# Four of a unit's sixteen gram copies on ScalarE are moved behind the copies of the second layer's sums

## The chip, the cores and the metric

The kernel runs as one program on one core of a Trainium2 chip. The metric is the device time of one execution in microseconds (us); lower is better. The engines are TensorE (PE in the profile, with PEld for its weight loads), VectorE (DVE), ScalarE (ACT), GpSimd (POOL) and SyncE (SP, which issues most transfers).

## What is computed

The reference chains three layers over 3072 tokens. Attention with a delta-rule state runs over 4 batches, 8 heads, 768 steps and 48 columns per head; a gated dense layer (384 to 1536 to 384) follows; a routed layer with eight experts and a skip test ends it. Cut to what matters:

```python
for t in range(S):                       # per batch and head, state [48, 48]
    y[t] = q[t] @ state
    v_old = state @ kn[t]                # kn: k, made unit length
    state = state + beta[t] * outer(kn[t], v[t] - v_old)

gate = sigmoid(x @ w_gate)               # x: y of all heads, [3072, 384]
x = (gate * (x @ w_val)) @ w_out

kept = x @ w_skip > 0                    # tokens that go through an expert
e = argmax(x @ w_gate2)                  # one of eight
out = x;  out[kept] += p_e * (relu(x @ w1[e]) @ w2[e])
```

All inputs and outputs are float32.

## The kernel before

The tokens are cut into 12 units of 256 tokens: 64 steps of each of the 4 batches. A loop over units `u` (in `program`, from 1 to 11) does, in each turn, twelve steps `f` of the dense layer of unit `u`, with the attention of later units and the routing of earlier ones woven in.

The dense layer, in each step: `first` (L863) multiplies the unit's x by the step's part of both up-weights into a PSUM tile gv (two buffers). `gate` takes it out: ACT makes sg, the sigmoid (L873), DVE multiplies it by the other half (L874), ACT rounds it to gh (L876), POOL makes the rest gl (L877). `second` (L886, L889) multiplies gh and gl by the out-weights and adds into two PSUM tiles acc, [128, 394] each, which are summed over all twelve steps. `second` runs two steps behind (`LAG = 2`). So the last two steps of unit `u - 1` come in steps 0 and 1 of unit `u`, and the first `second` of unit `u`, which overwrites acc, comes in step 2.

The routing of unit `u - 1` starts in step 1, behind that last `second` (in the first turn in step 0): ACT copies both acc tiles to x1 (L902, called x in the profile), POOL stores x1 to out (L896, two DMAs of 192 KB) and to xa (L923), and DVE works on it (L914 to L922 and, in step 3, L929 to L937).

The attention of unit `u + 2` starts in step 0 with `grams`: PE makes four PSUM tiles gram_0 to gram_3, all in one row of 64 matmuls (L300). ACT takes them out in the order 0, 2, 1, 3 with four copies each: two into g (L306), which SP then sends to DRAM as scr_g (L316), and two over the queries kq (L310), which POOL multiplies by a mask (L311). `blocks` brings scr_g back as bt (L331), and `solve` inverts small triangular blocks in it on DVE, in pieces that `spend` gives out over the steps; its last piece writes xx (L393). In step 0 of the next turn, the rest of an unfinished solve is run first. SP sends xx as scr_t (L397) and places it back as tt (L401, four DMAs). `combine`, in steps 2 to 4 of that turn, needs tt: DVE transposes it to dn (L588), PE multiplies to m1p (L594) and later to x2p (L604).

The masked kq are not read before `chain` of that unit, a turn later.

What sets the order: the loop is written under `in_order` for PE, DVE and ACT, so each of the three runs its instructions as a scheduler laid them out, from priority bands and a timeline, and waits for each in turn. SP and POOL have one queue each too. A wait holds all that stands behind it on that engine.

Of the kernel before, what the change touches and what calls it, by code (L numbers as in the profile page):

```python
# [17 lines left out]
AF = mybir.ActivationFunctionType  # L18
ALU = mybir.AluOpType
# [156 lines left out]
def sl(a, n):  # L176
    return slice(a, a + n)


class Attention:  # L180
# [90 lines left out]
    def keep(self, u, c, ps):  # L271

        nc = self.k.nc
        i, cc = divmod(c, 2)
        qp = self.u[u]["qp"][i]
        mask = self.k.c("mask").rearrange("p (a t) -> p a t", a=1).to_broadcast([128, 4, 64])
        for p, h in ((slice(64, 128), 0), (slice(0, 64), 1)):
            q = qp[p, cc, :, h, :]
            if u < KEEPA:
                nc.scalar.activation(q, ps[p, :, h, :], AF.Copy)  # L280
                nc.gpsimd.tensor_tensor(q, q, mask[p], op=ALU.mult)
            else:
                nc.vector.tensor_tensor(q, ps[p, :, h, :], mask[p], op=ALU.mult)

    def grams(self, u, tags):


        k, nc, p = self.k, self.k.nc, self.p
        d = self.u[u]
        g = d["g"] = p.tile([128, CPU_, 4, 64], F32, name=f"g{u}", tag="g", bufs=1)  # L290
        mask = k.c("mask").rearrange("p (a t) -> p a t", a=1).to_broadcast([128, 4, 64])
        for cc in range(2):
            ps = [k.ps_a.tile([128, 4, 2, 64], F32, name=f"gram{u}_{2 * i + cc}", tag=tags[2 * cc + i], bufs=1)
                  for i in range(2)]
            for pr in range(4):
                for i in range(2):
                    kt, kq = d["kt"][i], d["kq"][i]
                    for par in range(2):
                        r0, o0 = 64 * par, 64 * (1 - par if i == 0 else par)
                        nc.tensor.matmul(  # L300
                            ps[i][o0:o0 + 64, pr], kt[r0:r0 + 48, cc, pr, :], kq[r0:r0 + 48, cc, pr, par:par + 2],
                            start=True, stop=True)
            for i in range(2):
                for par in range(2):
                    r, o = sl(64 - 64 * par, 64), sl(64 * (1 - par if i == 0 else par), 64)
                    nc.scalar.activation(g[r, 2 * i + cc], ps[i][o, :, 1 - par, :], AF.Copy)  # L306
                for par in range(2):
                    r, o = sl(64 - 64 * par, 64), sl(64 * (1 - par if i == 0 else par), 64)
                    q = d["qp"][i][r, cc, :, par, :]
                    nc.scalar.activation(q, ps[i][o, :, par, :], AF.Copy)  # L310
                    nc.gpsimd.tensor_tensor(q, q, mask[r], op=ALU.mult)  # L311
        sg = self.scr_g[u % 2]
        for par in range(2):
            for blk in range(2):
                o0 = 64 * (1 - par) + 32 * blk
                nc.sync.dma_start(  # L316
                    sg[par, blk].rearrange("n m t -> m n t"),
                    g[o0:o0 + 32].rearrange("p c h t -> p (c h) t")[:, :, sl(32 * blk, 32)])

    def blocks(self, u, place=None, other=None):  # L320

        k, nc, p = self.k, self.k.nc, self.p
        d = self.u[u]
        if place is None:
            d["bt"] = p.tile([128, 32, 32], F32, name=f"bt{u}", tag="bt", bufs=1)
        else:
            d["bt"] = place
        first = None
        d["be"] = p.tile([128, 32], F32, name=f"be{u}", tag="be", bufs=2)
        for h2 in range(2):  # L330
            dma = (nc.sync, other or nc.sync)[h2].dma_start(  # L331
                d["bt"][sl(64 * h2, 64)], self.scr_g[u % 2].rearrange("r b n m t -> (r b n) m t"))
            first = first or dma
        for h2 in range(2):
            (other or nc.sync).dma_start(d["be"][sl(64 * h2, 64)], k.io["beta"][:, u])
        return first.ins
# [943 lines left out]
def drain(g):  # L1280
    for _ in g:
        pass
# [12 lines left out]
def program(ctx, tc, io, out):  # L1295
    k = Kernel(ctx, tc, io, out)
    k.setup()
    m1 = Moe1(k)
    xp = k.pool("xt")
    at = Attention(k)  # L1300
    dctx = ExitStack()
    m1.dp = k.pool("decode", ctx=dctx)
    nc = k.nc
# [221 lines left out]
    def between():  # L1525
# [10 lines left out]
        if GO == 0:  # L1536
            yield from grams(range(CPU_))
        early = third()
        for cs in ((0, 1), (2, 3)):
            if GO == 1:  # L1540
                yield from grams(cs)
            with k.band("prep"):
                for c in cs:
                    at.spread(1, c)
                gens = [at.double(1, c, k.ps_a, tags[(DT // 10, DT % 10)[c % 2]], 1) for c in cs]
            for _ in range(4):
                with k.band("prep"):
                    for g in gens:
                        next(g)
                yield  # L1550
            with k.band("prep"):
                turns(*gens)
            if GO == 2:
                yield from grams(cs)
# [51 lines left out]
    def spend(pieces, time):  # L1606

        pieces[1] += time
        with k.band("solve"):
            while pieces[1] > 0:  # L1610
                pieces[1] -= pieces[2]
                pieces[2] = next(pieces[0], 99)

    def load(u):
        with k.band("prep"):
            for i in range(2):
                at.load(u, i, (2 * u + i) % 4)

    def second():
        with k.band("second"):  # L1620
            m1.second(*behind.popleft())
# [3 lines left out]
    with k.in_order(*engines[0:3]):  # L1625
        for u in range(1, NU):
            more = u + 1 < NU
            if more:
                with k.band("top"):
                    xs[u + 1] = xp.tile([128, 2, KT3, UT], F32R, name=f"x{u + 1}", tag="x", bufs=2)  # L1630
                chain = at.chain(u + 1, xs[u + 1], "prep")
            join = at.combine(u + 1) if 2 < u + 1 < NU else iter(())
            route = m1.route(u - 1)
            for f in range(NF):
                with k.band("main"):
                    fp = m1.first(u, f, xs[u])
                with k.band("gate"):
                    g = m1.gate(*fp)
                    q = next(g)
                    drain(g)  # L1640
                if f == RANKF:
                    with k.band("route"):
                        drain(route)
                if f == GRAMF:
                    spend(solve, 99)
                if f == GRAMF and u + 2 < NU:
                    with k.band("prep"):
                        at.grams(u + 2, ("prep", "y", "rw", "s"))
                        at.blocks(u + 2)
                    solve = [at.solve(u + 2), 0, 1.1]  # L1650
                if f == JOINF - 1:
                    with k.band("prep"):
                        next(join, None)
                if f < JOINF or f > JOINF + 1:
                    spend(solve, SPEND[f])
                if more:
                    if f == JOINF:
                        with k.band("prep"):
                            next(join, None)
                        with k.band("top"):  # L1660
                            next(chain)
                    if f == JOINF + 1:
                        with k.band("prep"):
                            drain(join)
                if f in (JOINF, JOINF + 1):
                    spend(solve, SPEND[f])
                if more:
                    if f in WHEN:
                        with k.band("top"):
                            for _ in range(WHEN[f]):  # L1670
                                next(chain, None)
                    if f == LOADF and u + 3 < NU:
                        load(u + 3)
                    if f == LOADF and 2 < u + 2 < NU:
                        with k.band("prep"):
                            at.beside(u + 2)
                behind.append(q)
                if len(behind) > LAG:
                    second()
                if f == (LAG - 1 if u > 1 else 0):  # L1680
                    with k.band("route"):
                        next(route)
                        next(route)
            if u + 2 == NU:
                at.ctx.close()
                m2 = Moe2(k, m1)
        while behind:
            second()
# [114 lines left out]
```

## Time and profile before

| | |
|---|---|
| time, median of 3 runs | 933.21 us (931.25 to 935.35) |
| the profiled execution | 939.17 us, span 937.4 us |
| PE busy in the span | 843.2 us (90%) |
| DVE | 646.3 us (69%) |
| ACT | 424.4 us (45%) |
| POOL | 344.7 us (37%) |
| granted TensorE clock, mean | 0.962 |

The profiled execution is slower than the median of the unprofiled runs by some 6 us. The span is counted from its first instruction; the nine units that have grams start at about 206, 258, 310, 361, 411, 462, 514, 564 and 616, and the text calls a unit by that. In a timeline, a row is a time of start, a length, an engine, a line of the listing, what is written and read, and how many instructions were merged; the bracket at the end is the idle time of that engine before it and what ended that. A row without a bracket followed the one before it on its engine with no idle time worth naming. The share of busy time says little here: ACT is busy 45% of the time, and the rows are about one place where others stand behind it.

### The profile page before, as it was taken

The page shows a single profiled execution, that of the slowest core. Times are in us where ns is not written, and L with a number is a line of the kernel's source. Part 1 is how long each engine was busy: PE and PEld are TensorE (multiplying, and loading weights), DVE is VectorE, ACT ScalarE, POOL GpSimd, SP SyncE. Part 2 cuts the span into 40 slices and gives each one's busy share as a digit, 9 for nine tenths or more (in the row PEclk, how much of TensorE's full clock was granted, in tenths as well). Part 3 has the DMA queues.
Part 4 walks back from the last instruction along what each step waited for, and adds up shares of the span by engine and source line. Part 5 has one row for each costly group of instructions (what it writes and reads, how often), then busy time and mean ns, then how long its engine had stood idle before and what let it go on. Part 6 is the DMA issues. An engine that isn't in the chain of part 4 may idle for free.

```text
span 937.4 us, 26573 instructions
## 1 busy us (share of the span) xinstructions
PE 843.2 (90%) x10833; PEld 804.7 (86%) x10833; DVE 646.3 (69%) x1869; ACT 424.4 (45%) x998; POOL 344.7 (37%) x411
## 2 busy tenths in 40 slices
PE   6249797899889999999999999999899989999996
PEld 5247686789889999999989998999899988999996
DVE  6837785837959686878879796869622237877674
ACT  6365366354253535354443535353233235555452
POOL 6202564325261625344342616252322432412511
PEclk9999779779999999999999999999989999999999
DMA  8492303203343433333343434340200196766610
GB/s 191 138 366 84 80 2 111 51 3 76 77 107 81 103 81 64 86 68 86 83 103 78 109 78 104 84 101 15 61 3 15 48 340 202 252 206 218 213 55 15
DMA packets 132428, 99.29 MB, mean 106 GB/s; under 512 B 88231, under 2 KB 111868, under 8 KB 132304
## 3 DMA queue, kind: packets, MB, share of 16 engines
q1 hardware_dynamic: 125264, 78.44, 30.8%
q0 software_dynamic: 6624, 18.81, 6.6%
q8 instruction: 86, 1.41, 0.7%
q14 instruction: 38, 0.31, 0.1%
q10 hardware_dynamic: 416, 0.33, 0.1%
HBM read 76.66 MB, written 18.61 MB: 102 GB/s over the span
## 4 chain that ended last, share of the span: by engine, by line
PE 58%; DVE 17%; DMA 8%; ACT 7%; issue 6%; POOL 2%; SPq 2%; ACTq 0%; POOLq 0%; DVEq 0%
PE gv L863 22%; PE acc L886 9%; PE poe L1069 6%; PE he L1052 6%; PE acc L889 4%; DMA raw<-in_w 2%; ACT g L306 2%; DMA tt<-scr_t 2%; ACT kq L310 2%; PE y L714 2%; DVE tmp L386 2%; DVE sg L874 1%; DVE xx L391 1%; DVE dec L793 1%; PE x2p L604 1%
## 5 line engine op out<-in xcount | busy, mean ns | idle before, releaser
L863 PE MATMUL gv<-x,w 128*128 128x256 f32 x2592 | 349.1, 289 | 9.2 <-ACT w L802 3.6
L863 PEld LDWEIGHTS gv<-x,w 128*128 128x128 f32 x2592 | 339.6, 196 | 11.7 <-DVE sg L874 3.8
L877 POOL TENSOR_TENSOR gl<-sg,gh 128x256 fp32r<-128x256 f32 x144 | 114.2, 794 | 338.3 <-ACT gh L876 316.9
L886 PE MATMUL acc<-w,gh 128*128 128x394 f32 x576 | 138.7, 361 | 13.1 <-ACT x L902 8.1
L876 ACT ACTIVATE gh<-sg 128x256 fp32r<-128x256 f32 x144 | 60.2, 418 | 155.7 <-DVE sg L874 155.2
L874 DVE TENSOR_TENSOR sg<-sg,gv 128x256 f32<-128x256 f32 x144 | 60.0, 417 | 90.2 <-ACT sg L873 89.5
L873 ACT ACTIVATE sg<-gv 128x256 f32<-128x256 f32 x144 | 55.1, 383 | 139.3 <-PE gv L863 117.4
L886 PEld LDWEIGHTS acc<-w,gh 128*128 128x128 f32 x576 | 96.9, 192 | 20.5 <-ACT x L902 9.7
L386 DVE TENSOR_TENSOR tmp<-xx,bt 128x126 f32<-128x126 f32 (+28 forms) x299 | 95.7, 325 | 6.5
L391 DVE TENSOR_TENSOR xx<-xx,tmp 128x126 f32<-128x126 f32 (+28 forms) x299 | 87.3, 297 | 8.9
L889 PE MATMUL acc<-w,gl 128*128 128x394 f32 x288 | 77.8, 351 | 4.3 <-POOL gl L877 4.3
L971 DVE TENSOR_TENSOR w2le<-rawe,w2he 128x768 fp32r<-128x768 f32 x66 | 63.1, 955 | 10.6 <-ACT w2he L970 8.8
L311 POOL TENSOR_TENSOR kq<-kq,consts 64x256 f32<-64x256 f32 x72 | 55.5, 770 | 16.9 <-ACT kq L310 12.2
L889 PEld LDWEIGHTS acc<-w,gl 128*128 128x128 f32 x288 | 54.5, 194 | 5.0 <-POOL gl L877 4.9
L970 ACT ACTIVATE w2he<-rawe 128x768 fp32r<-128x768 f32 x66 | 55.4, 840 | 2.3 <-DMA rawe<-in_w 2.1
L803 POOL TENSOR_TENSOR w<-dec,w 128x576 fp32r<-128x576 f32 x24 | 31.5, 1330 | 62.2 <-ACT w L802 49.5
L1052 PE MATMUL he<-x2he,w2he 128*128 128x256 f32 x168 | 48.4, 288 | 1.9 <-DVE tgg L1159 1.4
L1060 ACT ACTIVATE hhe<-he 128x256 fp32r<-128x256 f32 x64 | 24.5, 383 | 50.6 <-PE he L1052 33.9
L1052 PE MATMUL he<-x2le,w2he 128*128 128x256 f32 x168 | 47.3, 282 | 0.0
L1052 PE MATMUL he<-x2he,w2le 128*128 128x256 f32 x168 | 47.1, 280 | 0.0
L1078 POOL DMA_INDIRECT out<-ote,tis x16 | 16.3, 1018 | 81.5 <-DVE ote L1077 77.1
L1069 PE MATMUL poe<-w2he,hhe 128*128 128x384 f32 x128 | 43.3, 338 | 0.0
(333 smaller groups left out, 1491.3 us busy)
## 6 DMA issues: line engine op xcount, KB each, us to landing
rawe<-in_w SPq DMA_DIRECT2D x64, 384.0 KB, 4.4
raw<-in_w SPq DMA_DIRECT2D x24, 576.0 KB, 6.2
kq<-in_kq SPq DMA_DIRECT2D x44, 192.0 KB, 5.1
kv<-in_kv SPq DMA_DIRECT2D x22, 384.0 KB, 5.9
xa<-x POOLq DMA_DIRECT2D x12, 392.0 KB
out<-x POOLq DMA_DIRECT2D x24, 192.0 KB
bt<-scr_g SPq DMA_DIRECT2D x18, 256.0 KB, 5.0
xx<-in_eye SPq DMA_DIRECT2D x9, 256.0 KB
```

The lines of the kernel that those rows point to most:

```text
L311: nc.gpsimd.tensor_tensor(q, q, mask[r], op=ALU.mult)
L386: v.tensor_tensor(t, x[:, :ni, m:m + 1].to_broadcast([128, ni, b - a]), bt[:, m:m + 1, m + 1 + a:m + 1 + b].to_broadcast([128, ni, b - a]) ...
L391: v.tensor_tensor(x[:, :ni, m + 1 + a:m + 1 + b], x[:, :ni, m + 1 + a:m + 1 + b], t, op=ALU.add)
L863: nc.tensor.matmul(gv[:, j], self.part(f, j, w)[:, c], y[:, a], start=n == 0, stop=n == 8)
L874: nc.vector.tensor_tensor(sg, sg, gv[:, 1], op=ALU.mult)
L876: nc.scalar.activation(gh, sg, AF.Copy)
L877: (nc.gpsimd if u < PG else nc.vector).tensor_tensor(gl, sg, gh, op=ALU.subtract)
L886: nc.tensor.matmul(self.acc[t], a[:, s], self.part(f, 2, b), start=f == 0 and n == 0, stop=False)
L889: nc.tensor.matmul(self.acc[t], gl[:, sl(128 * t, 128)], self.part(f, 2, 1), start=False, stop=f == NF - 1)
L971: nc.vector.tensor_tensor(l, raw, h, op=ALU.subtract)
L1052: nc.tensor.matmul(ps, ww[:, 0, s], xx[:, a], start=n == 0, stop=n == 8)
L1069: nc.tensor.matmul(po[t], a[:, s], b[:, 1], start=f == 0 and n == 0, stop=f == NF2 - 1 and n == 2)
```

## The change

`grams` becomes a generator. The copies of gram_1 and gram_3 into g stay where they were; the copies of these two over kq, and their products on POOL, are emitted after a `yield`. The loop runs the first part in step 0 as before, and the rest right after it has emitted the two x1 copies and the first half of the routing. `blocks` is emitted in between, as before.

```diff
--- before.py
+++ after.py
@@ -289,6 +289,14 @@
         d = self.u[u]
         g = d["g"] = p.tile([128, CPU_, 4, 64], F32, name=f"g{u}", tag="g", bufs=1)
         mask = k.c("mask").rearrange("p (a t) -> p a t", a=1).to_broadcast([128, 4, 64])
+
+        def keep(i, cc, ps):
+            for par in range(2):
+                r, o = sl(64 - 64 * par, 64), sl(64 * (1 - par if i == 0 else par), 64)
+                q = d["qp"][i][r, cc, :, par, :]
+                nc.scalar.activation(q, ps[i][o, :, par, :], AF.Copy)
+                nc.gpsimd.tensor_tensor(q, q, mask[r], op=ALU.mult)
+
         for cc in range(2):
             ps = [k.ps_a.tile([128, 4, 2, 64], F32, name=f"gram{u}_{2 * i + cc}", tag=tags[2 * cc + i], bufs=1)
                   for i in range(2)]
@@ -304,11 +312,8 @@
                 for par in range(2):
                     r, o = sl(64 - 64 * par, 64), sl(64 * (1 - par if i == 0 else par), 64)
                     nc.scalar.activation(g[r, 2 * i + cc], ps[i][o, :, 1 - par, :], AF.Copy)
-                for par in range(2):
-                    r, o = sl(64 - 64 * par, 64), sl(64 * (1 - par if i == 0 else par), 64)
-                    q = d["qp"][i][r, cc, :, par, :]
-                    nc.scalar.activation(q, ps[i][o, :, par, :], AF.Copy)
-                    nc.gpsimd.tensor_tensor(q, q, mask[r], op=ALU.mult)
+                if cc == 0:
+                    keep(i, cc, ps)
         sg = self.scr_g[u % 2]
         for par in range(2):
             for blk in range(2):
@@ -316,6 +321,9 @@
                 nc.sync.dma_start(
                     sg[par, blk].rearrange("n m t -> m n t"),
                     g[o0:o0 + 32].rearrange("p c h t -> p (c h) t")[:, :, sl(32 * blk, 32)])
+        yield
+        for i in range(2):
+            keep(i, 1, ps)
 
     def blocks(self, u, place=None, other=None):
 
@@ -1630,7 +1638,7 @@
                     xs[u + 1] = xp.tile([128, 2, KT3, UT], F32R, name=f"x{u + 1}", tag="x", bufs=2)
                 chain = at.chain(u + 1, xs[u + 1], "prep")
             join = at.combine(u + 1) if 2 < u + 1 < NU else iter(())
-            route = m1.route(u - 1)
+            route, grams = m1.route(u - 1), iter(())
             for f in range(NF):
                 with k.band("main"):
                     fp = m1.first(u, f, xs[u])
@@ -1645,7 +1653,8 @@
                     spend(solve, 99)
                 if f == GRAMF and u + 2 < NU:
                     with k.band("prep"):
-                        at.grams(u + 2, ("prep", "y", "rw", "s"))
+                        grams = at.grams(u + 2, ("prep", "y", "rw", "s"))
+                        next(grams)
                         at.blocks(u + 2)
                     solve = [at.solve(u + 2), 0, 1.1]
                 if f == JOINF - 1:
@@ -1681,6 +1690,8 @@
                     with k.band("route"):
                         next(route)
                         next(route)
+                    with k.band("prep"):
+                        drain(grams)
             if u + 2 == NU:
                 at.ctx.close()
                 m2 = Moe2(k, m1)
```

Nothing is added or taken away. On PE, DVE and SP the instructions stand in the same order as before. On ACT (g, kq: the gram copies; sg, gh: the gate; x: the copies of acc), in the unit that starts at 411, before:

```order
L306 ACTIVATE g_5797<-gram_1_5828 64x256 x2
L310 ACTIVATE kq_101<-gram_1_5828 64x4x64 x2
L306 ACTIVATE g_5797<-gram_3_5829 64x256 x2
L310 ACTIVATE kq_105<-gram_3_5829 64x4x64 x2
L873 ACTIVATE sg_1_5893<-gv_1_5874 128x256
L876 ACTIVATE gh_1_5894<-sg_1_5893 128x256
L902 ACTIVATE x_4_5906<-acc_0_5123 128x394
L902 ACTIVATE x_4_5906<-acc_1_5124 128x394
L873 ACTIVATE sg_2_5947<-gv_2_5928 128x256
```

and with the change (L314 is the old L306, L297 the old L310, L881 and L884 the old L873 and L876, L910 the old L902):

```order
L314 ACTIVATE g_5797<-gram_1_5828 64x256 x2
L314 ACTIVATE g_5797<-gram_3_5829 64x256 x2
L881 ACTIVATE sg_1_5885<-gv_1_5866 128x256
L884 ACTIVATE gh_1_5886<-sg_1_5885 128x256
L910 ACTIVATE x_4_5898<-acc_0_5123 128x394
L910 ACTIVATE x_4_5898<-acc_1_5124 128x394
L297 ACTIVATE kq_101<-gram_1_5828 64x4x64 x2
L297 ACTIVATE kq_105<-gram_3_5829 64x4x64 x2
L881 ACTIVATE sg_2_5947<-gv_2_5928 128x256
```

The four kq copies have moved past sg_1, gh_1 and the two x copies, and stand ahead of sg_2. In the first of the nine units they have moved past the two x copies and stand ahead of sg_1, because the routing comes in step 0 there. On POOL in the same place (gl: the gate's rest; out and xa: the stores), before:

```order
L311 TENSOR_TENSOR kq_101<-kq_101,consts 64x4x64 x2
L311 TENSOR_TENSOR kq_105<-kq_105,consts 64x4x64 x2
L311 TENSOR_TENSOR kq_101<-kq_101,consts 64x4x64 x2
L311 TENSOR_TENSOR kq_105<-kq_105,consts 64x4x64 x2
L877 TENSOR_TENSOR gl_1_5895<-sg_1_5893,gh_1_5894 128x256
L896 DMA out<-x_4_5906 64x2x384 x2
L923 DMA xa<-x_4_5906 128x2x392
L877 TENSOR_TENSOR gl_2_5949<-sg_2_5947,gh_2_5948 128x256
```

and with the change:

```order
L298 TENSOR_TENSOR kq_101<-kq_101,consts 64x4x64 x2
L298 TENSOR_TENSOR kq_105<-kq_105,consts 64x4x64 x2
L885 TENSOR_TENSOR gl_1_5887<-sg_1_5885,gh_1_5886 128x256
L904 DMA out<-x_4_5898 64x2x384 x2
L298 TENSOR_TENSOR kq_101<-kq_101,consts 64x4x64 x2
L931 DMA xa<-x_4_5898 128x2x392
L298 TENSOR_TENSOR kq_105<-kq_105,consts 64x4x64 x2
L885 TENSOR_TENSOR gl_2_5949<-sg_2_5947,gh_2_5948 128x256
```

Four of the eight products have moved past gl_1 and the out stores, two of them past the xa store too, and stand ahead of gl_2.

## Rows read from the trace of the kernel before

**Rows 1.** Waits by engine, 257 to 672: who waited for whom, total, times, longest.
```profile
PE acc L886 <- ACT x L902: 8.1, 8, 1.1
```

**Rows 2.** Timeline of PE, the unit at 411.
```profile
417.22 0.52 PE L889 MATMUL acc<-w,gl 128*128 128x394 f32 x2
...
420.86 1.02 PE L886 MATMUL acc<-w,gh 128*128 128x394 f32 x4 [0.99 <-ACT x L902]
...
424.43 1.20 PE L594 MATMUL m1p<-dn,g 32*32 32x32 f32 x64
```

**Rows 3.** Timeline of ACT, the unit at 411.
```profile
417.51 0.78 ACT L306 ACTIVATE g<-gram 64x256 f32<-64x256 f32 x2
418.32 0.79 ACT L310 ACTIVATE kq<-gram 64x256 f32<-64x256 f32 x2
...
420.32 0.87 ACT L902 ACTIVATE x<-acc 128x394 f32<-128x394 f32 x2
421.08 0.39 ACT L873 ACTIVATE sg<-gv 128x256 f32<-128x256 f32 x1
```

**Rows 4.** Timeline of SP's transfers, the unit at 411: start and length of the issue.
```profile
416.19 1.28 SPq L397 DMA_DIRECT2D scr_t<-xx  x2
417.91 1.97 SPq L316 DMA_DIRECT2D scr_g<-g  x4
419.99 1.49 SPq L401 DMA_DIRECT2D tt<-scr_t  x3
```

**Rows 5.** Timeline of DVE, the unit at 411 and the next one's first sg.
```profile
415.06 1.10 DVE L393 TENSOR_TENSOR xx<-xx,w 128x512 f32<-128x512 f32 x1
...
422.64 0.41 DVE L874 TENSOR_TENSOR sg<-sg,gv 128x256 f32<-128x256 f32 x1
423.46 0.77 DVE L588 STREAM_TRANSPOSE dn<-tt 128x256 f32<-128x256 f32 x2 [0.40 <-DMA tt<-scr_t]
...
462.15 0.42 DVE L874 TENSOR_TENSOR sg<-sg,gv 128x256 f32<-128x256 f32 x1
```

**Rows 6.** Timeline of SP, POOL, DVE and PE, the unit at 462.
```profile
470.62 1.66 SPq L401 DMA_DIRECT2D tt<-scr_t  x3
...
471.80 1.33 POOL L896 DMA_DIRECT2D out<-x  x2
...
475.31 0.77 DVE L588 STREAM_TRANSPOSE dn<-tt 128x256 f32<-128x256 f32 x2 [1.94 <-DMA tt<-scr_t]
...
475.81 1.20 PE L594 MATMUL m1p<-dn,g 32*32 32x32 f32 x64 [1.00 <-DVE dn L588]
```

**Rows 7.** Timeline of POOL, the unit at 411.
```profile
414.03 6.76 POOL L311 TENSOR_TENSOR kq<-kq,consts 64x256 f32<-64x256 f32 x8 [0.51 <-ACT kq L310]
...
421.49 1.33 POOL L896 DMA_DIRECT2D out<-x  x2
...
423.60 0.74 POOL L877 TENSOR_TENSOR gl<-sg,gh 128x256 fp32r<-128x256 f32 x1
```

**Rows 8.** DMA view, 421.3 to 422.7 (1.4 us): packets and rate of all queues.
```profile
DMA packets 1362, 0.17 MB, mean 121 GB/s; under 512 B 1362, under 2 KB 1362, under 8 KB 1362
```

**Rows 9.** DMA view, 426.2 to 426.8 (0.6 us); q0 carries POOL's store xa.
```profile
DMA packets 141, 0.23 MB, mean 380 GB/s; under 512 B 93, under 2 KB 94, under 8 KB 141
...
q0 software_dynamic: 45, 0.19, 86.1%
```

**Rows 10.** Timeline of DVE, the end of the first solve, before a POOL product begins.
```profile
256.10 0.69 DVE L393 TENSOR_TENSOR xx<-xx,w 128x512 f32<-128x512 f32 x1
```

**Rows 11.** Timeline of DVE and PE, the unit at 206.
```profile
213.64 0.17 DVE L914 TENSOR_REDUCE mx<-x 128x2 f32<-128x16 f32 x1 [12.30 <-ACT x L902]
...
215.11 0.41 DVE L874 TENSOR_TENSOR sg<-sg,gv 128x256 f32<-128x256 f32 x1
...
215.58 2.42 PE L863 MATMUL gv<-x,w 128*128 128x256 f32 x18 [0.58 <-DVE sg L874]
```

## The prediction

> **What bounds the kernel now.** I read in this order: the waits by engine, the timeline of the steady units engine by engine, then the DMA view of two short windows. Times are microseconds of the profiled execution (939.17, span 937.4); the median of the runs shown is 933.21. The sum below is a difference, put on the median.
>
> TensorE (PE) works all the time in the units and stops in one place: eight times it waits for ScalarE's copy of the finished sums, x from acc, 8.1 us together [rows 1]. One such place, in the unit that starts at 411: the old unit's last acc matmul ends at 417.22 + 0.52 = 417.74, but the first matmul of the new acc starts at 420.86 after 0.99 of idling, so PE wanted it at 419.87 [rows 2]. ScalarE could have copied from 417.74 on; it was in the last of the gram copies, and x came at 420.32 for 0.87 [rows 3]. That is the wait the change is aimed at.
>
> There is a second loop, which PE's idle time hardly shows. VectorE (DVE) solves the next unit's blocks up to xx (ends 415.06 + 1.10 = 416.16) [rows 5]; SP sends scr_t (416.19 to 417.47), then scr_g, which must have the last g copies, then tt from 419.99 [rows 4]; DVE's dn needs tt and starts at 423.46 after 0.40 of waiting [rows 5]; PE's m1p needs dn and starts at 424.43 [rows 2]. From dn on DVE runs its queue until the next unit's first sg at 462.15, which has no idle before it [rows 5]. So tt to dn, DVE's queue, xx, scr_t, tt closes a loop as long as PE's own. In the next unit it is the longer one: dn idles 1.94 for tt, and PE 1.00 for dn [rows 6]. A gain at x lasts only as far as tt comes earlier too.
>
> **What the change does, part by part.** Nothing is added or removed; PE, DVE and SP keep their order. In nine units four ScalarE copies (0.79 a pair, so 1.58) and four POOL products go behind the x copies and the stores.
>
> *x.* sg_1, gh_1 and x move up by 1.58: x from 418.74 to 419.61, which is after 417.74 and before 419.87. The wait of 0.99 goes, in eight units: 8.0 if nothing else held PE. The price on ScalarE is sg_2: it was at 421.08 [rows 3], and now stands behind the four copies, at 419.61 + 1.58 = 421.2. DVE takes sg_2 only at 422.64 [rows 5], so this costs nothing; were that cover gone, it would be 0.1.
>
> *scr_g and tt.* scr_g waits for the first of the last two g copies, now 0.79 earlier, but SP is in scr_t until 417.47, 0.44 before scr_g's start at 417.91 [rows 4]. So scr_g and tt can move up by 0.44 in five units; in the two at 310 and 564 the same rows leave the whole 0.8. In the unit at 258 dn does not wait for tt.
>
> *The products on POOL.* Eight run in one row until 420.79 [rows 7]; now four do, and the others come between and after the stores. The gl_2 behind them (423.60 [rows 7]) comes some 1.5 later; PE reads it two steps on. They now lie beside DVE's bound stretch. xx takes 1.10 beside a product [rows 5] and 0.69 where none runs when it starts [rows 10], so one DVE instruction caught costs 0.41: between 0 and 0.41 a unit. I take 0, because what stands there is dn, and two dn take 0.77 with a POOL product beside them [rows 5, 7] and without [rows 6].
>
> *The stores.* out follows x. It was issued at 421.49 [rows 7], 1.50 after the first tt; x being 1.58 earlier and POOL free, it goes out at 419.7, with tt at 419.55. So out and tt, apart before, meet on the DMA engines. What that costs, the trace of before doesn't show; two rows bound it. From below: nothing, if out's writes come late enough; then tt's 0.44 is kept. From above: the unit at 462, where tt and out were issued closest (470.62 for 1.66, and 471.80) and dn idled 1.94 in place of 0.40, 1.54 later [rows 5, 6]. Between them: tt's 128-byte pieces alone go through at 1362 in 1.4 us, 973 per us [rows 8]; beside the store xa the small ones come to 93 in 0.6 us, 155 per us, while xa moves 0.19 MB [rows 9]. At that rate the two out stores (192 KB each, 0.38 MB) take 1.2 us, in which tt loses 1.2 x (973 - 155) = 980 pieces, or 1.0 us. I take 1.0, since this row shows just such a meeting.
> The Trainium skill (DMA: Bandwidth & Descriptors, section Queues, rings and completion order) says that each DMA engine serves its queues in turn, a whole packet of typically 9 to 17 descriptors at a time; out would then hold tt for its whole 1.2 instead of 1.0, and the sum below would be 1.2 smaller. The trace agrees that both get turns.
>
> **The sum.** Per unit the gain is the lesser of what PE and what DVE can use.
> - Unit at 206: PE idles 0.58 for DVE's sg_1 (215.11), which stands behind the route work that began when x came (213.64) [rows 11]. x is 1.58 earlier: 0.6 (up to 1.5 if DVE's whole queue follows).
> - Unit at 258: 1.0.
> - The other seven: m1p can start 0.50 after dn (475.31 to 475.81 [rows 6]). At 411, m1p at 424.43 less (423.46 + 0.50) leaves PE 0.47, but DVE has no idle left before the next first sg: 0. The same two readings give 0 at 462 and 0.31, 0.26, 0.2, 0.6 and 0.13 in the others: 1.5 together. To this comes tt's own shift, one for one.
> - tt's shift: +1.0 - 0.44 = 0.6 later in four units, +1.0 - 0.8 = 0.2 later in two, and about 0.5 earlier at 462, where the meeting has been paid already: 2.3 later together.
>
> Gain 0.6 + 1.0 + 1.5 - 2.3 = 0.8 us. Later parts of the kernel take that over unchanged. The forecast is **932.4**, no change, where 0.5% (4.7 us) is about what a measurement of this kernel can tell from none. With tt's loss between 0.7 and 1.3, and the first unit at 1.5, this case alone spans 929.5 to 934.5.
>
> **The rivals.**
> 1. *Faster: out doesn't reach tt.* If out's writes start after tt's last, tt keeps 5 x 0.44 + 2 x 0.8 = 3.8 us. Sum 0.6 + 1.0 + 1.5 + 3.8 = 6.9: 926.3. For it: the wait is seen in eight units, and in most units before, tt and out kept apart. Against it: the two issues now lie within 0.2. Chance 0.28.
> 2. *Slower: each unit pays what the one at 462 pays.* tt is held for 1.5 us with the 0.44 lost in it, in six units, and DVE's loop carries it over: 9.2 less 3.1 is 6.1 slower, 939.3. The point is a shift of 3.1 / 7 = 0.44 per unit; over it the kernel is slower than before, and over 1.1 by more than 0.5%. For it: rows 6. Against it: in that unit only the end of tt met out, and its third tt issue took longer than others, so something else may have held it. Chance 0.14.
> 3. *The change does not reach x.* If x waits for another thing, such as the acc matmuls, the wait stays: 933.2. Against it: 417.74 is a microsecond ahead of 418.74. Chance 0.06.
>
> **How the numbers follow.** Forecast 0.52, rivals 0.28, 0.14 and 0.06. Faster by over 0.5% is rival 1 and a sliver of the forecast: 0.29. Within 0.5%: most of the forecast and rival 3, 0.57. Slower: rival 2, 0.14. The range reaches down to rival 1, with half a microsecond for the first unit (925.5), and up to 938.0, most of the way to rival 2; about a tenth is left out at each end.
>
> **What would show it.** Right: no wait of acc for x; the x copies 1.6 earlier in the unit and out within 0.3 of the first tt; dn's wait for tt grown from 0.40 to over 1, and PE idle before m1p in most units, where there was one. Rival 1: dn starts 0.4 or more earlier after xx than the 7.3 of before (416.16 to 423.46), and units get 0.5 shorter. Rival 2: dn 8.8 after xx everywhere, units longer than before. Wrong altogether: the wait at acc still there, or gv waiting for sg_2.

## The result, and the profile after

The change makes the kernel slower: 945.33 us (943.6 to 947.08) beside 934.17 (931.25 to 935.36) for the kernel before on the same chip, ratio 1.0136 with a 95% interval of 1.0113 to 1.0159. That is 11 us and outside the predicted range. The profiled execution took 945.28 us, span 943.5. Its lines are numbered some 8 higher than before; L314 and L297 are the g and kq copies, L904 the out stores.

The waits of PE in the steady units, 256 to 668 (columns: who waited for whom, total, times, longest), answer to [rows 1]:

```profile
PE m1p L602 <- DVE dn L596: 14.4, 7, 3.5
PE gv L871 <- issue: 1.4, 1, 1.4
PE acc L894 <- ACT x L910: 0.4, 1, 0.4
```

The 8.1 us of waiting for x are gone but for 0.4, as they should be. In their place PE waits for dn before m1p, seven times. The same unit as in [rows 2 to 7] now starts at 407; here are ACT, SP, POOL, DVE and PE of it, an engine to a fence, start and length first:

```profile
415.13 0.87 ACT L910 ACTIVATE x<-acc 128x394 f32<-128x394 f32 x2
416.03 1.59 ACT L297 ACTIVATE kq<-gram 64x256 f32<-64x256 f32 x4
```

```profile
412.58 1.28 SPq L405 DMA_DIRECT2D scr_t<-xx  x2
413.96 2.28 SPq L321 DMA_DIRECT2D scr_g<-g  x4
416.35 1.67 SPq L409 DMA_DIRECT2D tt<-scr_t  x3
```

```profile
416.30 1.33 POOL L904 DMA_DIRECT2D out<-x  x2 [0.19 <-issue]
417.70 1.54 POOL L298 TENSOR_TENSOR kq<-kq,consts 64x256 f32<-64x256 f32 x2
419.18 0.77 POOL L931 DMA_DIRECT2D xa<-x  x1
```

```profile
411.45 1.10 DVE L401 TENSOR_TENSOR xx<-xx,w 128x512 f32<-128x512 f32 x1
...
421.10 0.77 DVE L596 STREAM_TRANSPOSE dn<-tt 128x256 f32<-128x256 f32 x2 [2.62 <-DMA tt<-scr_t]
```

```profile
419.35 0.28 PE L936 MATMUL rank<-ob,consts_b 128*128 128x8 bf16 x5
421.60 1.48 PE L602 MATMUL m1p<-dn,g 32*32 32x32 f32 x64 [1.97 <-DVE dn L596]
423.01 1.96 PE L699 MATMUL ks<-sw,kq 48*64 48x48 f32 x64
...
430.18 1.20 PE L612 MATMUL x2p<-tt,g 32*32 32x32 f32 x64
```

Counted from xx's end (412.56 here, 416.16 before): x comes at 2.57 where it was 4.16, out goes at 3.74 where it was 5.33, and tt at 3.79 where it was 3.83. So out now stands on tt's issue. dn starts at 8.54 where it was 7.30, and PE idles 1.97. What follows on PE is the surprise: m1p takes 1.48 in place of 1.20, and from m1p to x2p it is 8.58 us in place of 5.61 (424.43 to 430.04 before). No wait stands in that stretch. The stretches of the timeline tell why; columns: window, length, busy time and instructions of PE, weight loads, DVE, ACT and POOL, **granted clock**, DMA share, GB/s.

```profile
371.00:374.50 3.50, 3.50 (x39) 3.41 (x30) 3.32 (x12) 1.60 (x3) 1.89 (x3) 0.51 0.25 79
...
412.50:421.00 8.50, 7.13 (x58) 6.99 (x56) 2.32 (x12) 5.66 (x15) 6.53 (x10) 1.00 0.79 164
421.00:422.30 1.30, 0.70 (x43) 0.70 (x45) 1.20 (x3) 0.00 (x0) 1.21 (x2) 0.99 0.98 242
422.30:429.10 6.80, 6.80 (x112) 6.64 (x106) 5.60 (x22) 2.39 (x5) 2.80 (x3) 0.50 0.32 99
429.10:436.00 6.90, 6.90 (x163) 6.54 (x162) 4.92 (x13) 2.25 (x5) 2.35 (x3) 1.00 0.14 23
...
476.90:483.70 6.80, 6.58 (x138) 6.42 (x139) 5.77 (x20) 2.39 (x5) 2.79 (x3) 0.50 0.35 83
531.50:538.30 6.80, 6.00 (x135) 5.85 (x136) 5.54 (x18) 2.39 (x5) 2.51 (x4) 0.50 0.33 104
592.90:596.30 3.40, 3.40 (x18) 3.38 (x13) 3.12 (x9) 1.41 (x3) 2.34 (x3) 0.51 0.15 24
640.70:644.10 3.40, 3.40 (x28) 3.31 (x21) 3.18 (x13) 1.59 (x3) 1.95 (x3) 0.51 0.36 100
```

Six times PE is granted half its clock, 1.2 GHz, for 3.4 to 6.8 us, 31 us together: five times in a stop for dn or up to 2.1 us behind its end (2.21, 1.97, 3.50, 3.35 and 1.89 long), and at 592.9 behind a stop of gv (1.45, with no other engine named). Two shorter stops for dn, 0.81 and 0.70, went without. In the six units with a fall m1p to x2p takes 7.12, 8.58, 8.42, 8.16, 7.22 (the 1.45 of gv among them) and 7.12 us. In the kernel before the same view says 1.00 from end to end of the steady units:

```profile
252.00:678.00 426.00, 410.15 (x6045) 398.20 (x6044) 332.83 (x1030) 186.78 (x460) 173.38 (x224) 1.00 0.36 82
```

The units show it too. The first two are shorter than before (49.70 and 49.92 us, from first sg to first sg, for 52.24 and 51.74); the six in which the clock falls take 52.4 to 55.3, where they took 50.2 to 51.8.

### The profile page after: what moved, and what is told of

Read it like the earlier page. It is cut to its first block, busy times and chain, and to the rows that moved or that the text cites. A ratio compares the mean times of both kernels' runs of the same rounds, so it can differ in the third digit from the quotient of the medians.

```text
span 943.5 us, 26605 instructions
## 1 busy us (share of the span) xinstructions
PE 845.1 (90%) x10833; PEld 808.5 (86%) x10833; DVE 650.9 (69%) x1869; ACT 424.4 (45%) x998; POOL 344.6 (37%) x411
## 4 chain that ended last, share of the span: by engine, by line
PE 56%; DVE 19%; DMA 9%; ACT 6%; issue 5%; SPq 3%; POOL 2%; ACTq 0%; POOLq 0%; DVEq 0%
PE gv L871 21%; PE acc L894 8%; PE poe L1077 6%; PE he L1060 6%; PE acc L897 4%; DMA tt<-scr_t 3%; ACT g L314 2%; DMA raw<-in_w 2%; DVE dec L801 2%; PE y L722 2%; DVE tmp L394 2%; DVE xx L399 2%; DVE sg L882 1%; PE ks L699 1%; PE m1p L602 1%
## 5 line engine op out<-in xcount | busy, mean ns | idle before, releaser
L894 PE MATMUL acc<-w,gh 128*128 128x394 f32 x576 | 141.5, 367 | 5.5 <-ACT w L828 3.2
L884 ACT ACTIVATE gh<-sg 128x256 fp32r<-128x256 f32 x144 | 60.2, 418 | 146.3 <-DVE sg L882 145.8
L881 ACT ACTIVATE sg<-gv 128x256 f32<-128x256 f32 x144 | 54.9, 381 | 145.2 <-PE gv L871 135.4
L894 PEld LDWEIGHTS acc<-w,gh 128*128 128x128 f32 x576 | 100.0, 197 | 10.9 <-issue 3.7
L897 PEld LDWEIGHTS acc<-w,gl 128*128 128x128 f32 x288 | 55.4, 197 | 5.3 <-POOL gl L885 5.2
L978 ACT ACTIVATE w2he<-rawe 128x768 fp32r<-128x768 f32 x66 | 55.4, 840 | 2.2 <-DMA rawe<-in_w 2.2
```

The lines of the kernel that those rows point to most:

```text
L884: nc.scalar.activation(gh, sg, AF.Copy)
L894: nc.tensor.matmul(self.acc[t], a[:, s], self.part(f, 2, b), start=f == 0 and n == 0, stop=False)
L897: nc.tensor.matmul(self.acc[t], gl[:, sl(128 * t, 128)], self.part(f, 2, 1), start=False, stop=f == NF - 1)
```

## The experiments

The theory they test: x early puts out on tt (step 1); tt and dn come late and PE idles before m1p (step 2); the clock falls behind that, and this is the larger part of the loss (step 3). Rivals: (A) the order of the g copies alone, by way of SP; (B) the late products on POOL; (C) PE runs denser without its waits for x, and the clock falls for that; (D) the wait is the loss, and the clock only follows.

The table has for each kernel the ratio to the kernel before on the same chip; and from one profiled execution dn's start after xx's end in the unit at 411, PE's waits for dn before m1p (200 to 668), and its time at half clock in the units from 258 on, by the stretches of 0.5 as above. The stop at some 680, in the last unit with a combine, is in every kernel, before too, and is left out of both; 3.4 to 10.2 us at half clock follow it, the most in the kernel before and in e10. Also left out are 3.4 us at half clock at some 247 in the kernel before, e1, e3 and e9. e6, e8 and e11 have four runs each, the change six, the others ten.

| kernel | ratio, 95% | dn after xx | waits | at half clock |
|---|---|---|---|---|
| before | 1 | 7.30 | 1.0 | 0 |
| the change | 1.0136 (1.0113, 1.0159) | 8.54 | 14.4 | 31 |
| e1 g order only | 1.0022 (0.9996, 1.0048) | 7.06 | 1.0 | 3 |
| e2 products, then stores | 0.9995 (0.997, 1.0019) | 7.35 | 7.3 | 20 |
| e3 stores a step later | 0.999 (0.9964, 1.0017) | 7.00 | 7.3 | 10 |
| e4 filled wait | 1.0014 (0.9987, 1.0041) | 8.82 | 5.0 | 0 |
| e5 later stores, fill of 8 | 0.9958 (0.9927, 0.9989) | 7.13 | 3.4 | 3 |
| e6 only xa later | 1.0104 (1.0061, 1.0146) | 8.73 | 16.1 | 34 |
| e7 only out later | 1.0027 (1.0008, 1.0045) | 7.32 | 7.5 | 14 |
| e8 fill elsewhere | 1.0175 (1.0147, 1.0203) | 8.52 | 11.4 | 14 |
| e9 before, fill of 8 | 1.0013 (0.9994, 1.0032) | 7.14 | 0.7 | 0 |
| e10 half of the copies | 1.0024 (0.9994, 1.0054) | 7.66 | 7.5 | 3 |
| e11 later stores, fill of 12 | 0.9911 (0.9877, 0.9946) | 7.11 | 1.0 | 0 |

**e1: the g order alone.** The four kq copies follow the last g copies at once, ahead of x:

```diff
-                        next(grams)
+                        drain(grams)
```

> One part of the change alone: the four last g copies stand together, but the four kq copies follow them at once, so x and the stores keep the place they had before the change. Theory (the loss comes from x and with it the out store moving up into tt): out is issued 1 us or more behind the first tt as before, dn starts about 7.0 to 7.5 after xx's end in the unit at 411, PE waits for x as before (7 to 8 us in all), the granted clock stays whole through the units; 930 to 935 us, ratio 0.995 to 1.001. Rival A (scr_g right behind scr_t slows SP's issues and so tt): scr_g's issue is 2.3 instead of 1.97, dn is 8.4 after xx's end and the clock falls in the units; 940 to 946 us, ratio 1.007 to 1.014.

Rival A falls: SP's issues are those of the change, dn is not late, and the time is that of before. In the same unit (SP, then DVE; xx ends at 412.50):

```profile
413.91 2.28 SPq L321 DMA_DIRECT2D scr_g<-g  x4
416.30 1.49 SPq L409 DMA_DIRECT2D tt<-scr_t  x3
```

```profile
419.56 0.77 DVE L596 STREAM_TRANSPOSE dn<-tt 128x256 f32<-128x256 f32 x2
```

It shows something else: scr_g starts 0.3 us earlier after xx than in [rows 4], and its issue takes as much longer (2.28 for 1.97), so tt goes at 3.80 and not at 3.4.

**e2 and e3: the stores behind tt.** e2 has POOL do the late products first, e3 the products and gl_2; nothing else moves. The edit of e2, cut to what matters:

```diff
                         next(route)
-                        next(route)
                     with k.band("prep"):
                         drain(grams)
+                    with k.band("route"), k.after(at.kept) if u + 2 < NU else ExitStack():
+                        next(route)
```

> The change, but POOL does the four late kq products ahead of the out and xa stores; ScalarE, VectorE, TensorE and SP keep the order of the change. Theory (the stores hold tt, dn comes late, PE idles before m1p and its clock falls): out goes about 2.5 to 3.4 us later than with the change, behind tt's last issue; dn is back to 7.0 to 7.5 after xx's end in the unit at 407, PE's waits for x stay away and those before m1p shrink to under 1 us, no fall of the clock; 925 to 931 us, ratio to the kernel before 0.990 to 0.997. Rival B (the late kq products on POOL, beside VectorE's bound stretch, are what costs): products still late, 940 to 946. Rival C (the clock falls because PE has lost its short waits for x and runs denser, whatever dn does): no waits for x, clock still falls, 940 or more.

> The change, but POOL issues the out and xa stores behind the gate's rest of the next step (gl_2), products and gl_2 before them; the order on all other engines is that of the change. Theory: as the run before, with gl_2 not delayed: dn 7.0 to 7.5 after xx's end, no fall of the clock in the units, 925 to 931 us, ratio 0.990 to 0.997. Rival B (late products): 940 to 946. Rival C (denser PE): clock still falls, 940 or more.

e3 (POOL and DVE, xx ends at 410.19):

```profile
414.16 3.23 POOL L298 TENSOR_TENSOR kq<-kq,consts 64x256 f32<-64x256 f32 x4 [0.45 <-ACT kq L297]
418.01 1.33 POOL L904 DMA_DIRECT2D out<-x  x2
```

```profile
417.19 0.77 DVE L596 STREAM_TRANSPOSE dn<-tt 128x256 f32<-128x256 f32 x2 [0.89 <-DMA tt<-scr_t]
```

The products run beside DVE as with the change, and the 11 us are gone: rival B falls, steps 1 and 2 stand. Neither kernel is faster than before, though, against what I expected. PE, which no longer waits for x, gets to m1p a microsecond sooner and waits there for dn instead, 7.3 us in all; in three units of each the clock still falls (in one of e2 it is nearer to a stop of ks, 1.43, with no engine named, than to the wait for dn). So the time that x gives goes into the wait for dn, and part of it into the clock. Rival C is not refuted by these two; e4 does that.

**e4 and e8: the wait filled.** Twelve matmuls on constants ahead of m1p, into the bank that m1p overwrites (e4); the same twelve ahead of x2p (e8). Both add these lines, with `FILL = 12`:

```diff
+        for _ in range(FILL):
+            nc.tensor.matmul(
+                ps.rearrange("p n t -> p (n t)")[:, 0:256], k.cb[:, 0:128], k.cb[:, 0:1].to_broadcast([128, 256]),
+                start=True, stop=True)
```

> The change, with twelve 128x256 matmuls on constants ahead of m1p in PE's queue (into the bank that m1p overwrites), so that PE works while dn is late; the stores still meet tt. Theory (the larger part of the loss is the halved clock after PE's idling, 2 to 3 us a unit in six or seven units): dn still 8.4 or later after xx's end, but the clock stays whole or falls for a shorter time, m1p to x2p back from 8.6 to under 6.5 us, and the time comes back to 931 to 938 us, ratio 0.997 to 1.004. Rival D (the wait itself and VectorE's loop are the loss, the clock only follows): m1p starts no earlier and the filling adds up to 1 us a unit; 945 to 952 us.

> Control for the filled wait: the same twelve matmuls, but ahead of x2p, some 5 us behind the wait, so PE idles before m1p as with the change. Theory (it is the idle time before m1p that makes the clock fall): waits of 1.5 to 3.5 before m1p, the clock falls in six or more units, 944 to 954 us, ratio 1.012 to 1.022. Rival F (any added PE work keeps the clock): clock whole, 931 to 938.

e4, PE in the unit where xx ends at 412.32, and the granted clock behind m1p:

```profile
418.89 1.49 PE L602 MATMUL m1p<-consts_b 128*128 128x256 bf16 x12
421.64 1.20 PE L607 MATMUL m1p<-dn,g 32*32 32x32 f32 x64 [1.25 <-DVE dn L597]
422.77 1.15 PE L704 MATMUL ks<-sw,kq 48*64 48x48 f32 x64
...
427.24 1.20 PE L617 MATMUL x2p<-tt,g 32*32 32x32 f32 x64
```

```profile
422.50:429.30 6.80, 6.80 (x179) 6.53 (x173) 5.87 (x22) 2.66 (x6) 2.81 (x3) 1.00 0.25 71
...
256.00:668.00 412.00, 406.25 (x5996) 393.94 (x5993) 328.33 (x1001) 181.74 (x450) 167.06 (x217) 1.00 0.35 82
```

e8, the same place, xx ends at 412.86:

```profile
421.87 1.20 PE L603 MATMUL m1p<-dn,g 32*32 32x32 f32 x64 [1.94 <-DVE dn L597]
423.00 1.52 PE L704 MATMUL ks<-sw,kq 48*64 48x48 f32 x64
424.45 1.68 PE L899 MATMUL acc<-w,gh 128*128 128x394 f32 x4
...
428.92 1.51 PE L611 MATMUL x2p<-consts_b 128*128 128x256 bf16 x12
```

These two bear on step 3 and on rivals C and D. In e4 out still meets tt, dn is late (8.45 to 9.06 in the four units from 361 to 514) and m1p starts no earlier in the unit shown, but m1p to x2p is 5.60, the clock is 1.00 in all of these units, and the kernel is back at the time of before (0.14% over it, interval -0.13% to 0.41%). By far most of the 1.36% goes with the halved clock. It is not quite the clock alone: with the change dn came at 10.07 and 9.93 in the units at 462 and 517, and in e4 at 8.50 and 9.06 in the same two. Over the six units in which the clock had fallen m1p starts 1.5 us earlier after xx in e4, all told, and m1p to x2p is 13.0 us shorter, 5.6 in each. PE runs denser in e4 than with the change, so density is not what lowers the clock (PE busy 406.25 of the 412 us, with the change 395.68 in the same window). The fill is not always enough: in the last unit with a combine, where 1.86 us of the wait are left in e4, 6.8 us at half clock follow.

In e8 the same work behind the wait gives nothing back, so it is not so that any added work keeps the clock. The work itself is on PE's path there, some 1.5 us a unit, so e8's time is not a price of the clock. Its falls in the units are three where I expected six or more, and waits of 1.82 and 2.22 went without one; whether the added work had a part in that, the runs don't show. The units with a fall take 53.8 to 55.4 us, the others 50.3 to 52.6.

**e6 and e7: which store.** One of the two store issues behind gl_2, the other where the change has it.

> The change, but of the stores only xa goes behind gl_2; out stays beside tt. Theory (out is the store that holds tt): dn still 8.2 or later after xx's end in most units, the clock falls, 939 to 946 us, ratio 1.007 to 1.014. Rival E (xa, issued beside tt's fourth transfer, is the larger part): dn 7.0 to 7.6, no fall, 929 to 934.

> The change, but of the stores only out goes behind gl_2; xa keeps its place between the late products. Theory (out holds tt): dn 7.0 to 7.5 after xx's end, at most three short falls of the clock, 929 to 934 us, ratio 0.997 to 1.002. Rival E (xa is the larger part): dn 8.0 or later, 938 to 946.

First e6 (xx ends at 417.67), then e7 (409.71), DVE of each:

```profile
426.40 0.77 DVE L596 STREAM_TRANSPOSE dn<-tt 128x256 f32<-128x256 f32 x2 [2.83 <-DMA tt<-scr_t]
```

```profile
417.04 0.77 DVE L596 STREAM_TRANSPOSE dn<-tt 128x256 f32<-128x256 f32 x2 [1.22 <-DMA tt<-scr_t]
```

It is out. With out beside tt dn is 8.73 after xx, without it 7.32, wherever xa is. e7's ratio, 1.0027, came out a little above the range I gave.

**e10: half the dose.** Only the last gram's two kq copies go behind x.

```diff
-                if cc == 0:
+                if cc == 0 or i == 0:
```

> Half the change: only the two kq copies of the last gram go behind the x copies, so x and out are about 0.8 us earlier than before in place of 1.6. Theory: out's first issue 4.5 after xx's end, between tt's third issue and its landing; dn between 7.4 and 8.3 after xx's end, waits before m1p up to 1.5, at most four falls of the clock; 933 to 940 us, ratio 1.001 to 1.009, between the kernel before and the change. If the loss had nothing to do with the stores' time but with the order of the g copies, it would be as before, 931 to 934.

Between the two as expected in time, though not told apart from no change: out goes 4.52 after xx, dn starts at 7.6 in three units, but in one at 8.5 and in two at over 9, later than I said.

**e5, e9 and e11: both costs taken away.** The stores of e3 and the fill of e4, with eight and with twelve matmuls; and the fill of eight in the kernel before.

> The stores a step later and eight matmuls on constants ahead of m1p: no part of the loss should be left. Theory: dn 7.0 to 7.4 after xx's end in most units, no fall of the clock in the units where the stores-later kernel still had three (3.4 us each at half, so 1 to 2 us each to win); 925 to 929 us, ratio to the kernel before 0.992 to 0.998. Rival (the fill takes what the early dn gave, since m1p starts behind it, and VectorE's loop bounds the units anyway): 930 to 934, ratio 0.998 to 1.003.

> The kernel before the change with the eight constant matmuls ahead of m1p and nothing else: what the fill is worth alone. There PE has no wait before m1p in most units and no fall of the clock in them, so theory: the fill's 1.05 us lies on PE's path where PE has about 0.5 to spare, 932 to 938 us, ratio 1.000 to 1.006; then what the kernel with later stores and fill gains comes from the early x copies. Rival G (the fill is the gain, the change is worth nothing even without its two costs): 925 to 929, ratio 0.993 to 0.997.

> The kernel with later stores and the fill, with twelve matmuls in place of eight: the last three units still had waits of 1 to 2 us and two falls of the clock. Theory: those falls go (1 to 2 us each), while the fill takes 0.45 us more in units where PE did not wait and VectorE's loop has that much cover: 924 to 929 us, ratio 0.991 to 0.997. Rival: the longer fill pushes m1p and costs as much, 928 to 932.

PE's wait for dn in e11, 200 to 700 (1.48 of it is the stop at some 680, so 1.0 is in the units):

```profile
PE m1p L607 <- DVE dn L597: 2.5, 2, 1.5
```

Both beat the kernel before: 927.4 us beside 932.19 (e5, 0.4% by the ratio), 927.13 beside 936.46 (e11, 0.9%). The fill alone shows no gain (e9), and neither do early copies with later stores but no fill (e3). In e9 PE still waits for x eight times, 8.0 us together, and in e11 not at all, which is about what lies between the two. So the early x copies look like the source of the gain, once what they set off is paid for. It is not shown outright: no run has the kernel before with later stores and fill together.

## Why the prediction was wrong

- **x's wait goes: right.** x 1.6 us earlier, the waits of [rows 1] gone, sg_2 and gl_2 free of cost, out within 0.05 us of the first tt.
- **"scr_g and tt can move up by 0.44": wrong.** They moved by 0.04 in the unit at 411, and by 0.5 to 0.6 in the two where I had 0.8. I read SP's gap ahead of scr_g as time to be had; scr_g's issue grew by what its start gained, and e1 shows the same without the rest of the change.
- **"I take 1.0" for what out takes from tt: too small.** dn is 1.24 later than before in the unit at 411 and 1.54 later than in e3. I had 1.0 less 0.44. Over the seven units from 310 on dn comes 0.3 earlier to 2.7 later than before, 7.0 us later together where I had 2.3. By the point that I gave in rival 2 (0.44 a unit) 7.0 over seven units already says slower, and in my own sum 7.0 less the 3.1 of gains is 3.9 us: the right sign and a third of the size, so the rest of the loss is not in this term. (At 462 SP came late to tt, so not all of it is out's.) How the pieces meet I had wrong as well, as the two DMA views below show.
- **What I left out: PE's clock.** The sum priced a late tt one for one. PE's idle time before m1p moved the clock, and that cost more than the late tt itself: m1p to x2p takes 13.0 us longer over the six falls than in e4, and these six units take 322.0 us together, in e4, with dn late too, 307.9, and before 305.4. The step that failed is "To this comes tt's own shift, one for one". The trace of before held the sign, outside the steady units: in the last unit with a combine dn waits for tt, PE stops for 2.93, and the granted clock is 0.5 for 10.2 us from 678.3 on (last views of this section). A stop of 2.59 for sg at 247 is followed by 3.4 us at half clock as well. In the steady units nothing warned: the one wait for dn, 1.00 in [rows 6], and the eight for x went without a fall.
- **"Stops in one place": not quite.** PE of before also stops for 1.84 (gv), 1.24 and 0.90 (x2p) and 1.00 (m1p); no term of the sum hangs on the first three.
- **DVE's loop: right**, and one reason why later stores alone gain nothing; the three falls of the clock in e3 are another. In e3 the three units from 305 to 456 take 50.4, 50.2 and 49.9 us, where they took 51.7, 50.2 and 50.3: the first gains, the other two hardly do, though PE no longer waits for x in them.
- **The first units: right in kind.** The wait of [rows 11] is gone; of one execution each, the first sg of the second unit comes 1.4 earlier and that unit is 2.5 shorter, where I had 0.6 and 1.0.
- **Rival 2 had the side, not the whole mechanism.** Its reading, that out beside tt is paid at the upper bound, is what e6 and e7 show.

The meeting of out and tt, [rows 8, 9] of now: the DMA view from 5.2 to 6.95 us after xx's end, first with the change, then in e3, where out comes later:

```profile
DMA packets 1000, 0.46 MB, mean 264 GB/s; under 512 B 917, under 2 KB 917, under 8 KB 1000
...
q0 software_dynamic: 102, 0.35, 63.1%
```

```profile
DMA packets 1411, 0.22 MB, mean 127 GB/s; under 512 B 1399, under 2 KB 1399, under 8 KB 1411
```

Beside out (q0) the small pieces of tt and bt still pass at 917 / 1.75 = 524 per us, not at the 155 of [rows 9]; but they fall 482 behind those of e3, and dn comes 1.5 later. The Trainium skill (DMA: Bandwidth & Descriptors, section Queues, rings and completion order) says that an engine takes its queues in turn by whole packets. The trace agrees that both go on together; that out holds tt for the whole of its own time, as I worked it out from that rule, it does not show.

The trace of before, in the last unit with a combine: dn, m1p, and a stretch with its granted clock, 0.93 in the mean because the 10.2 us at 0.5 lie in it:

```profile
678.64 0.77 DVE L588 STREAM_TRANSPOSE dn<-tt 128x256 f32<-128x256 f32 x2 [4.80 <-DMA tt<-scr_t]
```

```profile
679.18 1.92 PE L594 MATMUL m1p<-dn,g 32*32 32x32 f32 x64 [2.93 <-issue]
```

```profile
667.00:740.00 73.00, 69.56 (x762) 68.18 (x761) 19.71 (x69) 20.72 (x50) 21.51 (x29) 0.93 0.15 35
```

What stays open: why dn comes 8.1 to 10.0 after xx in one to three units of nearly every kernel in which out stays away from tt, before included [rows 6]. In one unit each of e2, e3 and e7 SP came to tt late (5.0 to 5.3 after xx): scr_g's issue took 2.8 to 3.5 us there, and tt's came 0.4 to 0.9 behind its end. The same happened with the change in the unit at 462. No run was made on that. Nor do the runs say which waits lower the clock: in e3 one of 0.81 was followed by a fall and one of 1.16 was not, and the stop for sg at some 246 was followed by one in the kernel before (2.59) and not with the change (2.67).

## What to carry to other kernels

An idle stop that is taken from PE's path at one place comes back at the next wait if a second loop is as long, so look where PE will stop next and what it did before that. A copy that comes earlier sends its store earlier: put the store behind the small-piece transfers that another engine waits for. Where a short wait of PE cannot be removed, work that does nothing is worth trying in it, when the rows behind the wait show the granted clock at half.

## What the hardware showed that was not expected

- In the steady units waits of PE of 0.8 to 3.5 us were followed by 3.4 to 6.8 us at 1.2 GHz, with PE at work in them nearly all the time; others of up to 2.2 us were not. With twelve 128x256 bf16 matmuls on constants (1.49 us) in the wait it stayed at 2.4 GHz, though up to 1.46 us of the wait were left; in the last unit, with 1.86 left, it did not.
- The time at half clock can exceed the wait: 6.8 us behind 1.97.
- Two 192 KB stores beside 128-byte pieces made the transfer's reader 1.2 to 1.5 us late, and the store xa in the same place did not.
- The issue of scr_g right behind scr_t took 2.28 us instead of 1.97 and ended as long after xx as before (3.7).
